# A fused sliding-window attention and gated feed-forward gradient kernel: score products two units ahead, transposed copies through DRAM, and other queues for the second half's loads

## The chip, the cores and the metric

The kernel runs on one core of a Trainium2 chip. The metric is the device time of one execution in microseconds (us). A core has TensorE (PE in the profile, with its weight loads apart as PEld), VectorE (DVE), ScalarE (ACT), GpSimd (POOL) and SyncE (SP). SP computes nothing here: it issues DMAs one after the other, and a DMA that has to wait for something holds back every DMA behind it on the same queue.

## The reference

The reference returns the output and all gradients of a gated sum of two branches, with 2048 positions, width 512 and bfloat16 data:

```python
g = sigmoid((x * gate_w).sum(-1, keepdims=True))
a = attention(x, wqkv, wo)       # 32 heads of 16, causal, window of 256 positions
b = (relu(x @ W_gate) * (x @ W_up)) @ W_down      # 1376 hidden columns
out = g * a + (1 - g) * b        # and the gradients to x, wqkv, wo, W_gate, W_up, W_down, gate_w
```

## The kernel before

The work has four parts in order of time.

**Prologue.** `x` and `grad_out` are loaded as rows and transposed on TensorE, the gate is computed, and `proj(0)` (L213) makes queries, keys, values and the projected output gradient of the first eight heads, which go through DRAM buffers `KV_d` and `QD_d`.

**Main loop** (L608 to L632). Eight groups of four heads times four blocks of 512 positions give 32 stages `n`. Each is visited twice: `A` with its queries against the keys in the window, and `N` with its keys against the queries. A visit has six units (L401): three packs of blocks, each for two heads of the four (`r` 0 or 1). This makes 384 units. A unit is: score matmuls into the PSUM tile `S` (L429), the exponential on ScalarE into `Pt` (L462), one or two mask instructions on GpSimd over `Pt` (L439), matmuls of the incoming gradient with the values into the PSUM tile `dP` (L429 too), and the product `Pd = Pt * dP` on VectorE (L467). `S` and `dP` have one buffer each. One step of the loop issues the `dP` matmuls of unit u woven with the `S` matmuls of unit u+1, then the exponential and masks of u+1, then the product of u. So the scores of a unit are one unit ahead of its product.

After the sixth unit of a visit the results are swept up on TensorE (L479) in small tasks (`tasks_A`, `tasks_N`), one per following step. `tasks_A` computes on VectorE `OB`, `Ar`, `V`, `tt`, on GpSimd `U`, `pr`, `dqO`, and turns `U` and `V` into rows with two transposing DMAs from SBUF to SBUF (L537, L538). `load_stage` (L377) loads the tiles of a later stage and transposes `kv` into `kvr` in the same way.

Each step also calls `fill` (L584). It takes one piece of a running `proj` (three of them are started, at `A` stages 0, 8 and 16) and as many pieces of the feed-forward part as keep that in step with the share of units done (`TOTAL` is its length in us as the code counts it). The feed-forward part works on 11 strips of 128 hidden columns (the last has 96). `ffn_front` (L243) makes, for each 512 positions, `rg` (ACT), `upm` (DVE), `hT` (POOL), `dhs` and `dgT` (DVE) and `duT` (POOL); it writes `hT`, `dgT`, `duT` to DRAM for the last part, and turns them into rows with 48 TensorE transposes per strip (L295) and six ScalarE copies `rw` (L296). `ffn_back` (L301) of the strip before reads those rows as matmul operands (L308, L318); the two generators alternate. The framework's scheduler then sets the order on each engine; it may move pieces past each other.

**Weight gradients of the attention** (L660 to L733, called part 5 below). Loads of `dqT`, `dkvT` and `OT` stand on SP's queue, and five weight loads on ScalarE's queue. 34 groups of TensorE transposes with a copy each (L685, L656, L658) turn the weights; then come four rounds of 16 tiles (L703).

**Output and input gradient** (L754 on, part 6): eight groups of two tiles, with `hT`, `dgT`, `duT` read back from DRAM.

## Time and profile before

| what | us |
|---|---|
| median of 4 runs (1236.8 to 1240.17) | 1238.53 |
| the profiled execution | 1245.8 |
| its span, first to last instruction | 1244.1 |
| before the first product | 50.6 |
| main loop, first to last product (50.6 to 891.6) | 841.0 |
| from there to the first matmul of the rounds (958.9) | 67.3 |
| the four rounds (to 1050.5) | 91.6 |
| part 6 (to the end) | 193.6 |

The profiled execution is 7.3 us above the median, and 1.7 us of its time lie outside its span. In a row of a group, `x` is the number of instructions, then busy time in us and the mean of one in ns, then the engine's idle time before them and what ended it. Rows of waits read "who <- for whom: us in total, times, longest". A chain of waits is followed back from the last instruction. `SPq` and `ACTq` are instructions that issue a DMA on SP's or ScalarE's queue: their time is that of the issue, not of the transfer.

### The profile page before, as it was taken

The numbers are of one execution on the slowest core, as the hardware profiler recorded it, in microseconds if no ns is written. First come the engines' busy times: TensorE is split into PE (matmuls) and PEld (weight loads), VectorE is DVE, ScalarE is ACT, GpSimd is POOL, SyncE is SP. The second block draws the span as 40 slices with busy tenths as digits, with TensorE's granted clock in tenths as the row PEclk, the third lists the DMA queues.
The fourth block names the chain that finished last, engine by engine and source line by source line (L and its number), as shares of the span: only waits on it lengthen the run. The fifth ranks groups of instructions, "written<-read, shape, count | busy, mean of one in ns | idle before, by whom it ended". The sixth has DMA issues, their size and how long they took to land.

```text
span 1244.1 us, 26168 instructions
## 1 busy us (share of the span) xinstructions
PE 1026.5 (83%) x10162; PEld 498.5 (40%) x10276; DVE 704.9 (57%) x876; ACT 619.7 (50%) x817; POOL 635.9 (51%) x1019
## 2 busy tenths in 40 slices
PE   5688888898788888888888888898706887899998
PEld 4234434444344343444434434344405443344443
DVE  2247777767677776678777776777402113223222
ACT  5256566675666666667676665666403222101110
POOL 2747766666676765667777665677401001122221
PEclk9889999899999999999999997999955999899999
DMA  7346232243232323323342332212395002834430
GB/s 194 90 121 148 76 87 65 58 125 87 68 88 65 89 71 98 103 60 87 76 90 63 72 83 65 65 36 53 100 233 207 17 18 77 243 102 151 126 102 22
DMA packets 191342, 117.57 MB, mean 95 GB/s; under 512 B 93489, under 2 KB 186066, under 8 KB 191218
## 3 DMA queue, kind: packets, MB, share of 16 engines
q1 hardware_dynamic: 160610, 89.78, 27.5%
q10 hardware_dynamic: 28224, 19.70, 5.6%
q0 software_dynamic: 2384, 6.43, 1.6%
q8 instruction: 80, 1.31, 0.4%
q14 instruction: 44, 0.36, 0.1%
HBM read 59.05 MB, written 44.21 MB: 83 GB/s over the span
## 4 chain that ended last, share of the span: by engine, by line
PE 34%; POOL 18%; DVE 15%; issue 10%; ACT 10%; DMA 9%; SPq 2%; ACTq 1%; DVEq 0%; POOLq 0%
DVE Pd L467 10%; POOL Pt L439 8%; PE dxps L804 7%; ACT Pt L462 4%; PE dP L429 4%; PE dw L719 4%; DMA dkvT<-DKV_d 3%; PE acc L479 3%; PE bps L771 2%; DMA duT_g<-duT_d 2%; PE mm L308 2%; POOL duT L287 2%; PE S L429 2%; POOL db_r L365 2%; POOL dqO L533 2%
## 5 line engine op out<-in xcount | busy, mean ns | idle before, releaser
L467 DVE TENSOR_TENSOR Pd<-Pt,dP 128x1024 bf16<-128x1024 bf16 (+2 forms) x384 | 442.6, 1153 | 199.7 <-POOL Pt L439 124.2
L462 ACT ACTIVATE Pt<-S 128x1024 bf16<-128x1024 f32 (+2 forms) x384 | 373.6, 973 | 228.8 <-PE S L429 201.0
L439 POOL TENSOR_SCALAR_AFFINE_SELECT Pt<-Pt 128x256 bf16<-128x256 bf16 (+1 forms) x736 | 347.4, 494 | 207.1 <-ACT Pt L462 203.9
L429 PE MATMUL dP<-dO,kv 32*128 32x128 bf16 (+2 forms) x704 | 77.0, 280 | 37.3 <-DVE Pd L467 33.2
L308 PE MATMUL mm<-rw,x_r 128*128 128x256 bf16 (+1 forms) x704 | 102.5, 277 | 0.8 <-ACT rw L296 0.8
L429 PE MATMUL dP<-kv,dO 32*128 32x384 bf16 (+2 forms) x704 | 73.5, 273 | 35.9 <-DVE Pd L467 33.6
L429 PEld LDWEIGHTS <-kv 32*128 32x128 bf16 x1408 | 47.0, 92 | 121.5 <-issue 112.5
L429 PE MATMUL S<-kv,Q 32*128 32x384 bf16 (+2 forms) x704 | 86.7, 275 | 6.8 <-ACT Pt L462 5.9
L778 ACT COPY a_sb<-aps 128x512 f32<-128x512 f32 x16 | 9.4, 586 | 161.3 <-issue 78.6
L429 PE MATMUL S<-Q,kv 32*128 32x128 bf16 (+2 forms) x704 | 84.1, 283 | 2.9 <-ACT Pt L462 1.6
L308 PEld LDWEIGHTS <-x_r 128*128 128x128 bf16 x704 | 61.5, 99 | 32.7 <-issue 21.0
L296 ACT COPY rw<-mmt 128x1024 bf16<-128x1024 bf16 (+1 forms) x66 | 65.1, 995 | 9.3 <-PE mmt L295 9.0
L804 PE MATMUL dxps<-WgT_sb,dgT_g 128*128 128x512 bf16 (+1 forms) x176 | 66.7, 379 | 0.8
L429 PEld LDWEIGHTS <-dO 32*128 32x128 bf16 x704 | 34.3, 91 | 79.3 <-issue 75.4
L711 POOL DMA_DIRECT2D go_t<-in_grad_out_dram x16 | 8.7, 544 | 112.1 <-DVE da_t L713 106.5
L287 POOL TENSOR_TENSOR duT<-dhs,rg 128x512 bf16<-128x512 bf16 (+1 forms) x44 | 54.3, 1235 | 17.4 <-DVE dhs L284 16.2
L804 PE MATMUL dxps<-WuT_sb,duT_g 128*128 128x512 bf16 (+1 forms) x161 | 61.0, 379 | 0.0
L277 POOL TENSOR_TENSOR hT<-rg,upm 128x512 bf16<-128x512 bf16 (+1 forms) x44 | 50.8, 1154 | 19.2 <-DVE upm L275 18.4
L227 PE MATMUL mm<-x_T,w 128*128 128x512 bf16 x180 | 51.0, 398 | 10.8 <-ACT cs L576 4.1
L719 PE MATMUL dw<-rt,x_r 128*128 128x512 bf16 x184 | 46.0, 387 | 12.3 <-ACT rt L656 11.8
L784 POOL DMA_DIRECT2D out_dram<-o_sb x16 | 8.7, 543 | 90.7 <-DVE o_sb L782 62.5
L782 DVE SCALAR_TENSOR_TENSOR o_sb<-bps,omg_all,ga 128x512 bf16<-128x512 f32 x16 | 12.0, 751 | 73.9 <-ACT ga L780 72.2
(155 smaller groups left out, 1686.3 us busy)
## 6 DMA issues: line engine op xcount, KB each, us to landing
hT_d<-hT SPq DMA_DIRECT2D x40, 128.0 KB
dgT_d<-dgT SPq DMA_DIRECT2D x40, 128.0 KB
duT_d<-duT SPq DMA_DIRECT2D x40, 128.0 KB
dgT_g<-dgT_d ACTq DMA_DIRECT2D x8, 640.0 KB
hT_g<-hT_d SPq DMA_DIRECT2D x8, 640.0 KB
duT_g<-duT_d ACTq DMA_DIRECT2D x8, 640.0 KB
KV_d<-cs SPq DMA_DIRECT2D x32, 128.0 KB
QD_d<-cs SPq DMA_DIRECT2D x32, 128.0 KB
```

What stands on the lines that cost most here:

```text
L227: nc.tensor.matmul(pp[:], lhsT=w3[:, cd, which, :], rhs=x_T[:, cd, sl], start=(cd == 0), stop=(cd == DC - 1))
L277: nc.gpsimd.tensor_tensor(out=hT[:fs, :], in0=rg[:fs, :], in1=upm[:fs, :], op=ALU.mult)
L287: nc.gpsimd.tensor_tensor(out=duT[:fs, :], in0=dhs[:fs, :], in1=rg[:fs, :], op=ALU.mult)
L296: nc.scalar.copy(rw[:, :, which, :fs], pt[:, :, :fs])
L308: nc.tensor.matmul(wps[:, 0:2 * fs], lhsT=x_r[:, t, c * P:(c + 1) * P], rhs=rows[t // 8][:, t % 8, 1:3, :fs], start=(t == 0), stop=(t == N ...
L429: lst.append(lambda lt=lt, ls=ls, rt=rt, rsl=rsl, i=i, rs=rs, col=col, cnt=cnt: nc.tensor.matmul(bank[:, i % 2, col * P:(col + cnt) * P], ...
L439: nc.gpsimd.affine_select(out=v.rearrange("p h (b k) -> p h b k", b=cnt), in_=v.rearrange("p h (b k) -> p h b k", b=cnt), compare_op=ALU.i ...
L462: nc.scalar.activation(u.Pt[:, :, :u.width], u.S[:, :, :u.width], ACT.Exp)
L467: nc.vector.tensor_tensor(out=u.Pd[:, :, :u.width], in0=u.Pt[:, :, :u.width], in1=u.dP[:, :, :u.width], op=ALU.mult)
L479: nc.tensor.matmul(acc[32 * i:32 * i + wt.shape[1], q0:q0 + cnt * P], lhsT=wt, rhs=m[:, i % 2, col * P:(col + cnt) * P], start=(fresh and ...
L719: nc.tensor.matmul(banks[c][:], lhsT=x_r[:, t, c * P:(c + 1) * P], rhs=rt[:].rearrange("p a b -> p (a b)"), start=(t == 0), stop=(t == NT ...
L804: nc.tensor.matmul(dxps[:], lhsT=l_, rhs=r_, start=(i == 0), stop=(i == len(pairs) - 1))
```

## The change

**Units.** The loop issues the scores two units ahead of the product: a step weaves `dP` of unit g-1 with `S` of unit g+1. The order of `r` in a visit becomes 0, 1, 1, 0, 0, 1 and is mirrored in every other visit; the two units of a step then use different rows of the TensorE array, as they did before. `Pt` has 10 buffers for 9; `U`, `V` and `OB` one for two. `S` and `dP` keep one buffer each.

**Feed-forward rows.** The TensorE transposes and their ScalarE copies are gone. `hT`, `dgT`, `duT` are written to one DRAM tensor `ffn_d`, and right behind the three writes one transposing DMA reads a 384 x 512 block of it back as rows (three of 96 x 512 each in the last strip). It has to wait until the three writes have landed. `TOTAL` goes from 262 to 229.

**Attention rows.** `U` and `V` are written to DRAM (`UV_d`), and one transposing DMA reads both back; `kvr` is made from `KV_d` in DRAM and not from `kv` in SBUF.

**Pacing.** A running `proj` gives a piece at every second step, not at every one, and its `cs` has four buffers for two. `load_stage(n + 2)` comes one step later, behind the product.

**Part 5.** The five weight loads move from ScalarE's queue to SP's; three stand ahead of `dqT`, and `Wd` and `wo` behind `OT`.

```diff
-            for hf in range(NSB // 2):
...
-                rw = fp.tile([P, 8, 3, P], BF, tag="rows", bufs=3)
-                for which in range(3):
-                    pt = tr_bank(8)
-                    for k in range(8):
-                        nc.tensor.transpose(pt[:, k, :fs], parts[k // 4][which][:fs, (k % 4) * P:(k % 4 + 1) * P], ident[:fs, :fs])
-                    nc.scalar.copy(rw[:, :, which, :fs], pt[:, :, :fs])
+            for tg in range(NSB):
...
+                for w, src_t in enumerate((hT, dgT, duT)):
+                    nc.sync.dma_start(ffn_d[fc, w, :fs, sl], src_t[:fs, :])
+                rw = fp.tile([P, 4, 3, P], BF, tag="rows", bufs=6)
+                if fs == P:
+                    nc.sync.dma_start_transpose(out=rw[:].rearrange("p k w f -> p k (w f)"),
+                                                in_=ffn_d[fc, :, :, sl].rearrange("w p s -> (w p) s"))
+                else:
+                    for w in range(3):
+                        nc.sync.dma_start_transpose(out=rw[:, :, w, :fs], in_=ffn_d[fc, w, :fs, sl])
...
-            transpose_rows(kvr, kv)
+            nc.sync.dma_start_transpose(out=kvr[:], in_=KV_d[c][sb][half * P:(half + 1) * P, :])
...
-                transpose_rows(RU, v.U)
-                transpose_rows(RV, v.V)
+                nc.sync.dma_start(UV_d[n][0], v.U[:])
+                nc.sync.dma_start(UV_d[n][1], v.V[:])
+                R = ap_.tile([P, 4, 2, P], BF, tag="R", bufs=3, name="R")
+                nc.sync.dma_start_transpose(out=R[:].rearrange("p k w f -> p k (w f)"),
+                                            in_=UV_d[n].rearrange("w p s -> (w p) s"))
...
         def fill(frac):
-            if projs:
+            turn[0] += 1
+            if projs and turn[0] % 2:
...
-            lists = second(u)
-            if nxt is not None:
-                lists = lists + first(nxt)
+            lists = (second(cur[4]) if cur else []) + (first(nxt[4]) if nxt else [])
             weave(lists)
             if nxt is not None:
-                after_scores(nxt)
-            product(u)
+                after_scores(nxt[4])
+            if cur is not None:
+                kind, n, us, j, u = cur
+                product(u)
...
-            nc.scalar.dma_start(Wg_sb6[:], B_W_gate.rearrange("(c p) f -> p c f", p=P))
-            nc.scalar.dma_start(Wu_sb6[:], B_W_up.rearrange("(c p) f -> p c f", p=P))
-            nc.scalar.dma_start(wqkv_sb6[:], A_wqkv.rearrange("(c p) n -> p c n", p=P))
+            nc.sync.dma_start(Wg_sb6[:], B_W_gate.rearrange("(c p) f -> p c f", p=P))
+            nc.sync.dma_start(Wu_sb6[:], B_W_up.rearrange("(c p) f -> p c f", p=P))
+            nc.sync.dma_start(wqkv_sb6[:], A_wqkv.rearrange("(c p) n -> p c n", p=P))
```

What this does to the order on the engines shows at three places. The first is VectorE in the middle of the main loop. Numbers are given to tiles in the order in which the code makes them. Before, `Pt_7022` is made just before the product `Pd_7026` and read by the very next product:

```order
L467 TENSOR_TENSOR Pd_7026<-Pt_6994,dP_7012 128x1024
L275 SCALAR_TENSOR_TENSOR upm_7071<-rg_7010,mm_7066 128x512
L467 TENSOR_TENSOR Pd_7057<-Pt_7022,dP_7043 128x1024
L467 TENSOR_TENSOR Pd_7102<-Pt_7053,dP_7088 128x1024
L467 TENSOR_TENSOR Pd_7152<-Pt_7098,dP_7138 128x1024
```

In the change `Pt_8057` is made just before `Pd_8060`, and another product stands between that and the one that reads it:

```order
L462 TENSOR_TENSOR Pd_8060<-Pt_7949,dP_8049 128x1024
L504 SCALAR_TENSOR_TENSOR OB_8099<-acc_8062,vec_154,ri_8003 128x512
L462 TENSOR_TENSOR Pd_8097<-Pt_7973,dP_8087 128x2x256
L462 TENSOR_TENSOR Pd_8132<-Pt_8057,dP_8122 128x2x256
L270 SCALAR_TENSOR_TENSOR upm_8141<-rg_8047,mm_8136 128x512
```

`Pt` moved one product further ahead; `dP` is still made for the next product alone.

The second place is SP's queue in the main loop. Before, writes, loads and single-block transposes alternate, and none of them reads what another of them has just written to DRAM:

```order
L534 DMA DQO_d<-dqO 128x512
L385 DMA Q_4_597<-QD_d_2_82 16x512 x2
L381 DMA kv<-KV_d_2_66 128x512
L386 DMA dO_4_602<-QD_d_2_82 16x512 x2
L289 DMA hT_d<-hT 128x512
```

In the change the transposing read `rw<-ffn_d` follows the last write of its block, `dgT`, with four small loads between:

```order
L284 DMA ffn_d<-duT 128x512
L284 DMA ffn_d<-dgT 128x512
L380 DMA Q_0_623<-QD_d_2_112 16x512 x4
L287 DMA_TRANSPOSE rw<-ffn_d 128x4x384
L532 DMA UV_d_65<-V 128x512
L172 DMA wg<-in_B_W_gate_dram 128x4x128
```

Whatever stands behind that read on the queue now waits until the write has landed.

The third place is ScalarE's queue where part 5 begins. Before, its first copy of transposed weights stands behind the issue of all five loads (`Wd` in two pieces):

```order
L674 DMA Wg_sb_15073<-in_B_W_gate_dram 128x4x1376
L323 CAST dst<-mm 96x512
L675 DMA Wu_sb_15074<-in_B_W_up_dram 128x4x1376
L676 DMA wqkv_sb_15075<-in_A_wqkv_dram 128x4x1536
L677 DMA Wd_sb_15047<-in_B_W_down_dram 128x10x512
L679 DMA Wd_sb_15047<-in_B_W_down_dram 96x512
L680 DMA wo_sb_15050<-in_A_wo_dram 128x4x512
L656 COPY WgT_sb<-pt 128x512 x5
```

In the change no load stands ahead of that copy on ScalarE, and SP's queue reads:

```order
L668 DMA dqT<-DQO_d 128x1x2048
L663 DMA Wg_sb_14501<-in_B_W_gate_dram 128x4x1376
L664 DMA Wu_sb_14502<-in_B_W_up_dram 128x4x1376
L665 DMA wqkv_sb_14503<-in_A_wqkv_dram 128x4x1536
L668 DMA dqT<-DQO_d 128x1x2048 x2
L670 DMA dkvT<-DKV_d 128x2048 x8
```

The loads of part 5 moved from two queues to one, with two of the four pieces of `dqT` ahead of the weights.

More of the change, by code (lines that the diff above doesn't have):

```diff
@@ L317, in ffn_back @@
             for t in range(NT):
-                nc.tensor.matmul(dps[:fs, :D], lhsT=rows[t // 8][:, t % 8, 0, :fs], rhs=db_r[:, t, :],
+                nc.tensor.matmul(dps[:fs, :D], lhsT=rows[t // 4][:, t % 4, 0, :fs], rhs=db_r[:, t, :],
                                  start=(t == 0), stop=(t == NT - 1))
@@ L549, in f @@
                     d, k = divmod(a - 4 * sb, 4)
[L550 removed]
+                    return st["rn", n + d][:, k, which, 32 * i:32 * i + width]
                 return f
@@ L576, in act_copy @@
             nc.scalar.copy(out, in_)
-        slots = sum(len(units(k, n)) for k, n in order)
         dense = {"done": 0.0, "t": 0.0}
         ffn = ffn_all()
-        TOTAL = 262.0
+        TOTAL = 229.0
         projs = []
+        turn = [0]
         def fill(frac):
-            if projs:
+            turn[0] += 1
+            if projs and turn[0] % 2:
                 try:
@@ L597 @@
             load_stage(n)
[L598 to L601 removed]
         seq = []
[L603 removed]
+        for kind, n in order:
+            us = units(kind, n)
             for j, u in enumerate(us):
                 seq.append((kind, n, us, j, u))
[L606 to L611 removed]
+        pending = []
+        for g in range(-1, len(seq) + 1):
+            nxt = seq[g + 1] if g + 1 < len(seq) else None
+            cur = seq[g - 1] if g >= 1 else None
+            if nxt is not None and nxt[0] == "A" and nxt[3] == 0:
+                n = nxt[1]
+                if n % 8 == 0 and n // 8 + 1 < DC:
                     projs.append(proj(n // 8 + 1, act_copy))
@@ L658, in evac @@
                 nc.vector.tensor_copy(out, in_)
-        dqo_v = DQO_d.rearrange("(c g w d) s -> w c g d s", c=DC, g=8, w=2)
-        for c in range(DC):
-            nc.sync.dma_start(dqT[:, c, :], dqo_v[0, c])
-        for hg in range(NHG):
-            nc.sync.dma_start(dkvT[:, hg, :], DKV_d[hg * P:(hg + 1) * P, :])
-        for c in range(DC):
-            nc.sync.dma_start(OT[:, c, :], dqo_v[1, c])
         with ExitStack() as p5:
```

165 lines of the change are left out of this document (75 added, 90 removed).

## The prediction

> **What bounds the kernel now.** I read the stretches first, cut at the first product, the last product and the first and last matmul of the rounds. Columns are start:end, length, then busy time of PE, PEld, DVE, ACT and POOL, then the granted TensorE clock, the DMA share and GB/s.
>
> ```profile
> 50.60:891.60 841.00, 720.70 (x8453) 344.99 (x8538) 609.78 (x660) 545.51 (x693) 558.03 (x918) 0.98 0.31 80
> 891.60:958.90 67.30, 23.42 (x176) 18.37 (x176) 8.44 (x21) 12.12 (x22) 7.81 (x11) 0.57 0.85 234
> 958.90:1050.50 91.60, 75.16 (x493) 40.31 (x503) 22.32 (x51) 21.26 (x38) 4.86 (x9) 0.98 0.11 35
> 1050.50:1244.10 193.60, 177.04 (x787) 76.80 (x800) 52.15 (x115) 19.61 (x34) 36.70 (x48) 0.98 0.40 123
> ```
>
> Part 6 keeps PE busy 91% of its time, and the change gives it the same matmuls and the same row lengths: I leave its 193.6 us and the rounds' 91.6 as they are. What is left is the main loop, where no engine is full, and the 67.3 us behind it, where PE works a third of the time.
>
> In the loop I asked who waits for whom.
>
> ```profile
> POOL Pt L439 <- ACT Pt L462: 203.9, 203, 4.5
> ACT Pt L462 <- PE S L429: 201.0, 229, 3.9
> DVE Pd L467 <- POOL Pt L439: 124.2, 151, 5.4
> PE dP L429 <- DVE Pd L467: 66.8, 155, 1.7
> ```
>
> That is a ring: the product waits for the masks, these for the exponential, this for the scores; and the scores are woven with `dP` matmuls that wait for the product before. Since the scores are one unit ahead, the ring closes over two products. If I remove it, the next ring is the short one of `dP` alone, and VectorE's timeline shows its length.
>
> ```profile
> 833.37 1.22 DVE L467 TENSOR_TENSOR Pd<-Pt,dP 128x1024 bf16<-128x1024 bf16 x1 [0.58 <-PE dP L429]
> 834.51 0.74 DVE L517 SCALAR_TENSOR_TENSOR Ar<-acc,vec,ri 128x512 f32<-128x512 f32 x1
> 835.17 0.68 DVE L275 SCALAR_TENSOR_TENSOR upm<-rg,mm 96x512 bf16<-96x512 bf16 x1
> 835.76 1.21 DVE L467 TENSOR_TENSOR Pd<-Pt,dP 128x1024 bf16<-128x1024 bf16 x1
> ...
> 841.12 1.21 DVE L467 TENSOR_TENSOR Pd<-Pt,dP 128x1024 bf16<-128x1024 bf16 x1
> 842.25 0.74 DVE L528 SCALAR_TENSOR_TENSOR tt<-acc,vec,OB 128x512 f32<-128x512 f32 x1
> 842.91 1.22 DVE L467 TENSOR_TENSOR Pd<-Pt,dP 128x1024 bf16<-128x1024 bf16 x1
> ```
>
> A product cannot follow the one before by less than 0.58 us, while `dP` is refilled. One other operation fits into that gap (841.12 to 842.91 is 1.79, less 1.21 is 0.58); two make it 1.18 (833.37 to 835.76, less 1.22), and I take 2.0 for three or more by the same spacing. `dP` keeps its one buffer, so this floor stays.
>
> **The floor and the room above it.** The products themselves:
>
> ```profile
> L467 DVE TENSOR_TENSOR Pd<-Pt,dP 128x1024 bf16<-128x1024 bf16 (+2 forms) x384 | 442.6, 1153 | 199.7 <-POOL Pt L439 124.2 <-PE dP L429 40.2 <-PE S L429 24.0
> ```
>
> In the change's order on VectorE, of the 383 gaps between products 185 are empty, 134 hold one operation, 55 two and 9 more. The floor is 442.6 + 319 x 0.58 + 55 x 1.18 + 9 x 2.0 = 711 us, or 1.85 per product. The loop takes 841, so its whole room is 130 us. Where that lies shows when the same stretches are asked for the products alone (length, then DVE busy and count of products, clock, DMA share, GB/s; a product across a border counts twice):
>
> ```profile
> 50.60:128.00 77.40, 27.78 (x25) 0.93 0.49 123
> 128.00:226.00 98.00, 55.20 (x48) 1.00 0.29 75
> 226.00:282.50 56.50, 27.72 (x25) 0.94 0.37 96
> 282.50:436.30 153.80, 82.99 (x73) 0.99 0.31 80
> 436.30:547.60 111.30, 55.30 (x49) 1.00 0.32 85
> 547.60:741.80 194.20, 110.61 (x96) 1.00 0.33 77
> 741.80:798.30 56.50, 27.67 (x24) 0.82 0.23 60
> 798.30:891.60 93.30, 55.29 (x48) 1.00 0.18 48
> ```
>
> With 24, 48, 24, 72, 48, 96, 24 and 48 products at 1.85, the excess is 33, 9, 12, 21, 22, 17, 12 and 4 us. The start has 33. The stretches with a running `proj` (the third, the head of the fourth, the fifth) have about 45. The seventh has 12 at a granted clock of 0.82. Plain stretches have about 40.
>
> **The change part by part.**
>
> *Scores two units ahead.* The exponential:
>
> ```profile
> L462 ACT ACTIVATE Pt<-S 128x1024 bf16<-128x1024 f32 (+2 forms) x384 | 373.6, 973 | 228.8 <-PE S L429 201.0
> ```
>
> The long ring then closes over three products. Its own length, from the end of a product: 0.97 for the exponential and 1.22 for the product by their rows, and as my estimates 0.5 for the scores, 1.0 for two masks and 0.3 of handing over, about 4.0: 2.0 per product over two, 1.33 over three, below the 1.8 of the short ring. So the mask waits go, and the `dP` wait is late next. POOL is the releaser of 124.2 of the 199.7 us for which VectorE idles, but of each such wait 0.58 would be there anyway. In the plain stretches I take half of the 40 back (bounds 0 and 35): -22. At the start the loads of the first stages bind as well: -15 of 33 (0 to 25).
>
> *Pacing of `proj`, four `cs` buffers.* A ScalarE copy into `cs` waits for the write two copies before, on the engine that makes the exponentials. In the chain two such writes stand whole:
>
> ```profile
> 72.63 3.12 DMA KV_d<-cs
> 498.06 2.63 DMA QD_d<-cs
> ```
>
> They run from issue to landing. With four buffers and half the pace a write has four times as long, and the wait goes: -27 of the 45 (10 to 35). The clock dip I leave in, since nothing in the change speaks to it.
>
> *TensorE transposes and their copies gone.* Rows of the loop stretch for L295 (PE, PEld) and the group of L296:
>
> ```profile
> 50.60:891.60 841.00, 46.49 (x528) 33.27 (x528) 0.98 0.31 80
> L296 ACT COPY rw<-mmt 128x1024 bf16<-128x1024 bf16 (+1 forms) x66 | 65.1, 995 | 9.3 <-PE mmt L295 9.0
> ```
>
> PE loses 46.5 us and ACT 65.1, but both are idle for over 100 us of the loop now, and neither is the floor: 0 by itself, and part of what makes the terms above possible.
>
> *Rows through DRAM.* Two costs, both on SP. First its time. Median issues now (min/median/max in ns):
>
> ```profile
> L396 SPq DMA_TRANSPOSE RU<-U x32: 1189/1192/1945, 84.3 to 859.3; - x32
> L289 SPq DMA_DIRECT2D hT_d<-hT x44: 304/358/956, 75.0 to 875.7; - x44
> L388 SPq DMA_DIRECT2D qd<-QD_d x32: 327/571/1436, 46.4 to 787.5; - x32
> ```
>
> Up to part 5 the change's order has 732 plain DMAs and 116 transposes of 225 blocks of 128 x 512 (before: 669 and 96). Some 690 plain ones fall into the loop, at 0.45 (between the rows) 310 us. No row shows a transpose out of DRAM: from below it is a plain issue, 116 x 0.36 = 42; from above it is 1.19 for every block, 268. Then 84 groups of transposes wait for their own writes, 2.6 to landing less the issues between, at most 1.8 each: 150. The sum is 450 to 728 of a loop of 785. I take the upper end, since the only transposes in the trace cost 1.19: SP stays hidden, without reserve. The Trainium skill (Advanced Engine Details and Errata, X-Bar Transpose) says that transposing DMAs are as fast as regular ones on this chip. For the issue the row speaks against it, 1.19 to 0.36; by the rule SP's sum would be the lower end and the time the same.
>
> Second, latency. By the change's order five other units' `dP` stand on PE between the last gradient matmul of a strip (it feeds `dhs`) and the first matmul that reads the rows of that last block: 5 x 2.0 = 10 us.
>
> ```profile
> L287 POOL TENSOR_TENSOR duT<-dhs,rg x44: 1148/1156/1414, 75.4 to 876.4; 128x512 bf16<-128x512 bf16 x40, 96x512 bf16<-96x512 bf16 x4
> ```
>
> In that time must pass `dhs` (0.68), a wait for a product (0.6), `duT` (1.16), SP's queue (0.5), the write (2.6 to 3.1) and the transposing read (2.6 as a plain one, 5.8 with two more block issues): 8.1 to 11.8 us. What is missing stalls PE and all that stands behind it there, `dP` first: 0 to 2 us on each of 10 strips. I take 8 of 0 to 20.
>
> *Attention rows, `load_stage` one step later, fewer `U`, `V`, `OB` buffers.* 0: the rows of `U` and `V` are read some 12 units after the transpose is issued, over 20 us, and the loads serve a stage two ahead. If SP fell behind, this cover would go too; that is a rival below.
>
> Loop: 841 - 22 - 15 - 27 + 8 = 785.
>
> *Part 5.* TensorE's timeline behind the loop:
>
> ```profile
> 894.68 1.89 PE L318 MATMUL mm<-db_r,rw 128*96 128x512 bf16 x8
> ...
> 902.68 1.01 PE L685 MATMUL pt<-ident,Wg_sb 128*128 128x128 bf16 x8 [6.11 <-DMA Wg_sb<-in_B_W_gate_dram]
> ```
>
> and that of all engines and queues:
>
> ```profile
> 899.72 40.77 SPq L664 DMA_DIRECT2D dkvT<-DKV_d  x8
> ...
> 919.97 0.37 ACTq L677 DMA_DIRECT2D Wd_sb<-in_B_W_down_dram  x1
> ...
> 937.20 0.44 ACTq L680 DMA_DIRECT2D wo_sb<-in_A_wo_dram  x1
> 937.68 1.07 ACT L656 COPY WgT_sb<-pt 128x512 bf16<-128x512 bf16 x2 [40.50 <-DMA dkvT<-DKV_d]
> ...
> 957.68 1.01 PE L685 MATMUL pt<-ident,dqT 128*128 128x128 bf16 x8 [0.25 <-ACT wkvT L656]
> ```
>
> ScalarE's first copy comes at 937.68 behind the issue of `wo`, 40.5 us late; the 34 groups then take 20 us (937.7 to 957.7). In the change ScalarE issues nothing here. Counted from 896.6, where PE ends the loop's leftovers: ahead of `Wg` stands half of `dqT` (1.0 MB), then `Wg` 1.4, `Wu` 1.4, `wqkv` 1.6 MB. At 234 GB/s they are there after 11, 17 and 24 us. GpSimd's reordering of `wqkv` takes 4 us, the last eight groups 5: rounds from 33, now 62 (958.9). The half of `dqT` left needs 4 us more of transfer, by 28: in time. Bounds 10 (a copy still waits for a late transfer) to 32; I take 26.
>
> Sum: 1245.8 - 56 - 26 = 1163.8; less 7.3, by which the profiled execution lies above the median, 1157.
>
> **The rivals.** (a) *The rows come late.* Stalls of 5 us and more per strip take back the loop's whole gain; part 5 alone stays: 1238.5 - 26 = 1212. For it: the path needs up to 11.8 of 10 us. Against it: only the last block of a strip is tight, the third has 13 units. (b) *Part 5 is bound by transfers.* 67.3 us at 234 GB/s are 15.7 MB, the same bytes after. If the first copies still wait for late pieces, only the loop gains: 1157 + 26 = 1183. The Trainium skill (DMA: Bandwidth & Descriptors, Issuing engines are not separate DMA queues) has it that the DMAs of all queues share the same engines, and that another queue saves issue time alone. Against it: what ScalarE waited for at 937.68 was not the weights, and PE had `Wg` at 902.7. (c) *SP becomes the bound, slower.* If a block out of DRAM costs 2.0 us of SP's time and not 1.19, the queue needs 310 + 450 + 150 = 910 us, the loads come late and the loop follows: +69 - 26, 1281. It decides from 1.8 a block (310 + 150 + 225 x 1.8 = 865, 24 above the loop of now). For it: the upper sum has no reserve, and a transposing issue took up to 1.9 us now and then (`RU`, above). Against it: DRAM reads as such issue in 0.36 to 0.57. (d) *Nothing comes of it:* the new waits eat all, 1238.
>
> **How the numbers follow.** Forecast 0.60, (a) 0.14, (b) 0.10, (c) 0.13, (d) 0.03. The range goes from 1110, where the loop comes within 25 us of its floor, to 1225, beyond (a): outside lie (c), (d) and a little below, under 2 in 10. About 0.2% is what a measurement can tell from no change. Faster 0.84, same 0.03, slower 0.13.
>
> **What would show it.** Right: VectorE's waits for POOL's masks nearly gone, `dP` in their place, products 1.80 apart in plain stretches; 384 products in some 785 us; the first `WgT` copy about 12 us and the rounds about 33 us after PE's last loop matmul. Wrong: transposing issues on SP well over 1.2 us a block, or waits of L303 for `rw` in the tens of us, or `S` and the exponential still releasing the product.

## The result and the profile after

| | us |
|---|---|
| before, median of 15 runs | 1242.38 |
| changed, median of 11 runs (1142.7 to 1155.08) | 1153.06 |
| ratio, 95% interval | 0.9266 (0.9235 to 0.9296) |
| changed, profiled execution (span 1141.0) | 1142.7 |

The forecast was 1157 in a range of 1110 to 1225. The profiled execution lies 10 us below the median; how executions of one kernel differ is taken up at the last experiment. First the stretches of the changed kernel, cut at the same events as before: first product, last product, first and last matmul of the rounds.

```profile
49.80:817.90 768.10, 679.32 (x7892) 312.63 (x8002) 611.87 (x656) 486.73 (x624) 554.86 (x918) 0.99 0.48 120
817.90:856.70 38.80, 18.86 (x151) 15.50 (x150) 8.52 (x22) 11.61 (x20) 7.84 (x11) 0.56 0.89 281
856.70:948.70 92.00, 75.18 (x494) 39.98 (x503) 22.64 (x52) 21.76 (x39) 4.86 (x9) 0.98 0.27 85
948.70:1141.00 192.30, 177.77 (x784) 76.93 (x800) 51.67 (x115) 19.11 (x33) 36.70 (x48) 0.97 0.40 124
```

The loop went from 841.0 to 768.1 (785 forecast), the stretch behind it from 67.3 to 38.8 (41.3 forecast); the other two stayed within 1.3 us. VectorE is busy in the loop as long as before, 612 us beside 610; the time came out of its gaps. Who waits for whom in the changed kernel:

```profile
ACT Pt L457 <- PE S L424: 178.7, 243, 3.5
POOL Pt L434 <- ACT Pt L457: 140.6, 167, 4.3
DVE Pd L462 <- PE dP L424: 70.3, 110, 3.5
DVE Pd L462 <- PE S L424: 37.6, 47, 8.7
DVE Pd L462 <- POOL Pt L434: 10.1, 12, 1.7
```

The product's wait for the masks fell from 124.2 to 10.1. ScalarE and GpSimd still wait long, 178.7 and 140.6, but now a unit ahead, where the product seldom stands right behind them. What is late next is `dP`, as forecast. The waits put down to `S` grew from 24.0 to 37.6; 38 of the 47 are no longer than 0.65 us, which is the gap of the short ring (the scores are woven with `dP` in one step), and one, of 8.7, belongs to late rows and comes up again at `hybrid_last`. VectorE's timeline in the middle of the loop shows the short ring at its length:

```profile
565.17 1.22 DVE L462 TENSOR_TENSOR Pd<-Pt,dP 128x1024 bf16<-128x1024 bf16 x1 [0.60 <-PE dP L424]
566.97 1.22 DVE L462 TENSOR_TENSOR Pd<-Pt,dP 128x1024 bf16<-128x1024 bf16 x1 [0.58 <-PE dP L424]
568.11 0.68 DVE L270 SCALAR_TENSOR_TENSOR upm<-rg,mm 128x512 bf16<-128x512 bf16 x1
568.74 1.22 DVE L462 TENSOR_TENSOR Pd<-Pt,dP 128x1024 bf16<-128x1024 bf16 x1
```

Starts are 1.80 and 1.77 apart, with and without another operation in the gap. Now the products alone, in stretches that hold the same products as the eight of before (columns as there):

```profile
49.80:113.30 63.50, 27.61 (x24) 0.92 0.63 156
113.30:207.60 94.30, 55.27 (x48) 1.00 0.52 127
207.60:255.70 48.10, 27.64 (x24) 1.00 0.52 134
255.70:397.00 141.30, 82.95 (x73) 1.00 0.50 122
397.00:497.30 100.30, 55.23 (x49) 1.00 0.49 126
497.30:678.10 180.80, 110.51 (x96) 1.00 0.48 119
678.10:723.50 45.40, 27.61 (x24) 1.00 0.48 117
723.50:817.90 94.40, 55.24 (x48) 0.98 0.29 71
```

| stretch | before | after | |
|---|---|---|---|
| start | 77.4 | 63.5 | -13.9 |
| second | 98.0 | 94.3 | -3.7 |
| third, `proj` | 56.5 | 48.1 | -8.4 |
| fourth, `proj` at its head | 153.8 | 141.3 | -12.5 |
| fifth, `proj` | 111.3 | 100.3 | -11.0 |
| sixth | 194.2 | 180.8 | -13.4 |
| seventh, clock 0.82 before | 56.5 | 45.4 | -11.1 |
| eighth | 93.3 | 94.4 | +1.1 |

SP's transposing issues, whose price the prediction could only bound (min/median/max in ns), for three blocks, two and one of 128 x 512:

```profile
L287 SPq DMA_TRANSPOSE rw<-ffn_d x40: 1293/1414/2322, 69.4 to 730.8; - x40
L534 SPq DMA_TRANSPOSE R<-UV_d x32: 1232/1251/2863, 83.9 to 789.0; - x32
L385 SPq DMA_TRANSPOSE kvr<-KV_d x32: 1194/1208/2032, 49.5 to 691.3; - x32
```

At the median one such issue costs 1.21 us for one block, 0.04 more for two and 0.20 more for three. With the last strip's 12 (median 1.19) all 116 come to 40 x 1.41 + 32 x 1.25 + 32 x 1.21 + 12 x 1.19 = 149 us, where the prediction had 42 to 268 and took 268.

Part 5, all engines and queues behind the loop:

```profile
825.10 0.40 SPq L663 DMA_DIRECT2D Wg_sb<-in_B_W_gate_dram  x1
...
833.96 1.01 PE L681 MATMUL pt<-ident,Wg_sb 128*128 128x128 bf16 x8 [15.46 <-DMA Wg_sb<-in_B_W_gate_dram]
834.63 0.59 ACT L653 COPY WgT_sb<-pt 128x512 bf16<-128x512 bf16 x1 [15.24 <-PE pt L681]
```

ScalarE's first copy now comes 0.7 us behind the first transpose, and not behind the issue of five loads; the transposes wait 15.5 us for `Wg`.

### The profile page after: what moved, and what is told of

Its sections match the earlier page's. It is cut to its first block, busy times and chain, and to the rows that moved or that the text cites. A ratio compares the mean times of both kernels' runs of the same rounds, so it can differ in the third digit from the quotient of the medians.

```text
span 1141.0 us, 25063 instructions
## 1 busy us (share of the span) xinstructions
PE 984.7 (86%) x9607; PEld 465.1 (41%) x9748; DVE 709.7 (62%) x876; ACT 562.7 (49%) x751; POOL 632.7 (55%) x1019
## 3 DMA queue, kind: packets, MB, share of 16 engines
q8 instruction: 76, 1.25, 0.5%
## 5 line engine op out<-in xcount | busy, mean ns | idle before, releaser
L457 ACT ACTIVATE Pt<-S 128x1024 bf16<-128x1024 f32 (+2 forms) x384 | 372.6, 970 | 197.2 <-PE S L424 178.7
L434 POOL TENSOR_SCALAR_AFFINE_SELECT Pt<-Pt 128x256 bf16<-128x256 bf16 (+1 forms) x736 | 348.0, 496 | 146.5 <-ACT Pt L457 140.6
L303 PE MATMUL mm<-rw,x_r 128*128 128x256 bf16 (+1 forms) x704 | 102.2, 274 | 10.3 <-DMA rw<-ffn_d 10.0
L424 PEld LDWEIGHTS <-kv 32*128 32x128 bf16 x1408 | 55.7, 92 | 114.6 <-issue 104.9
L424 PE MATMUL dP<-dO,kv 32*128 32x128 bf16 (+2 forms) x704 | 74.3, 273 | 27.4 <-DVE Pd L462 24.5
L424 PE MATMUL S<-kv,Q 32*128 32x384 bf16 (+2 forms) x704 | 78.5, 276 | 2.6 <-ACT Pt L457 1.4
L424 PE MATMUL S<-Q,kv 32*128 32x128 bf16 (+2 forms) x704 | 78.1, 275 | 2.8 <-ACT Pt L457 1.9
L303 PEld LDWEIGHTS <-x_r 128*128 128x128 bf16 x704 | 60.6, 98 | 44.8 <-issue 31.5
L424 PEld LDWEIGHTS <-dO 32*128 32x128 bf16 x704 | 30.1, 92 | 72.3 <-issue 69.2
L779 POOL DMA_DIRECT2D out_dram<-o_sb x16 | 8.7, 542 | 90.1 <-DVE o_sb L777 62.4
L715 PE MATMUL dw<-rt,x_r 128*128 128x512 bf16 x184 | 45.9, 387 | 12.7 <-ACT rt L653 12.2
L282 POOL TENSOR_TENSOR duT<-dhs,rg 128x512 bf16<-128x512 bf16 (+1 forms) x44 | 51.4, 1168 | 6.9 <-DVE dhs L279 6.4
L225 PE MATMUL mm<-x_T,w 128*128 128x512 bf16 x175 | 48.6, 386 | 3.9 <-issue 1.9
L653 ACT COPY rt<-pt 128x512 bf16<-128x512 bf16 x32 | 18.8, 588 | 65.7 <-PE pt L681 65.7
```

The lines of the kernel that those rows point to most:

```text
L225: nc.tensor.matmul(pp[:], lhsT=w3[:, cd, which, :], rhs=x_T[:, cd, sl], start=(cd == 0), stop=(cd == DC - 1))
L282: nc.gpsimd.tensor_tensor(out=duT[:fs, :], in0=dhs[:fs, :], in1=rg[:fs, :], op=ALU.mult)
L303: nc.tensor.matmul(wps[:, 0:2 * fs], lhsT=x_r[:, t, c * P:(c + 1) * P], rhs=rows[t // 4][:, t % 4, 1:3, :fs], start=(t == 0), stop=(t == N ...
L424: lst.append(lambda lt=lt, ls=ls, rt=rt, rsl=rsl, i=i, rs=rs, col=col, cnt=cnt: nc.tensor.matmul(bank[:, i % 2, col * P:(col + cnt) * P], ...
L434: nc.gpsimd.affine_select(out=v.rearrange("p h (b k) -> p h b k", b=cnt), in_=v.rearrange("p h (b k) -> p h b k", b=cnt), compare_op=ALU.i ...
L457: nc.scalar.activation(u.Pt[:, :, :u.width], u.S[:, :, :u.width], ACT.Exp)
```

## The experiments

The theory is the prediction's: a ring of masks, exponential and scores over two products bound the loop, writes of `cs` held `proj`, and ScalarE's issues held part 5; transposes on TensorE and their replacement are off the path. The rivals: the transposes made the gain; part 5 is bound by transfers; SP or the rows come close to binding. Ratios are to the kernel before, on the same chip in the same rounds. The changed kernel itself was timed in a second set as well, `same_again`:

> The changed kernel as it is, for a second profile on the chip of the two below: 1148 to 1157. Its first profiled execution took 1142.7, 10 under the median of 1153. If that was the clock, this one shows more stretches of granted clock 0.5 in the loop, and as much more time there; if it was something else, the loop is longer at the same clock.

It gave a median of 1146.51, ratio 0.9234 (0.9202 to 0.9266), and a profile of 1145.0 with a loop of 770.0: as fast as the first profile, so that it left the question open which it was meant for. Where a run is set against the changed kernel below, that counts as the mean of the two ratios, 0.925, and a difference of ratios is turned into us by 1240.

| run | median | ratio, 95% interval | against changed |
|---|---|---|---|
| `one_ahead` | 1192.38 | 0.9635 (0.9594 to 0.9675) | +48 |
| `pe_rows` | 1151.14 | 0.9321 (0.9280 to 0.9362) | +9 |
| `proj_old` | 1169.40 | 0.9446 (0.9416 to 0.9477) | +24 |
| `cs_two` | 1159.72 | 0.9334 (0.9301 to 0.9367) | +10 |
| `act_loads` | 1178.14 | 0.9499 (0.9466 to 0.9532) | +31 |
| `act_three` | 1166.22 | 0.9403 (0.9373 to 0.9433) | +19 |
| `split_three` | 1182.06 | 0.9523 (0.9489 to 0.9558) | +34 |
| `hybrid_last` | 1153.92 | 0.9298 (0.9254 to 0.9341) | +6 |
| `part5_chain` | 1137.20 | 0.9185 (0.9151 to 0.9220) | -8 |
| `b_two_ahead` (from before) | 1202.05 | 0.9703 (0.9677 to 0.9730) | |
| `b_part5` (from before) | 1215.31 | 0.9778 (0.9743 to 0.9813) | |

**`one_ahead`**: the distance of the scores undone.

```diff
-            for k, r in enumerate((0, 1, 1, 0, 0, 1)):
+            for k, r in enumerate((0, 1, 0, 1, 0, 1)):
...
-                u.kind, u.n, u.p, u.r, u.width, u.base = kind, n, k // 2, r ^ (stage_no["n"] % 2), width * P, base
+                u.kind, u.n, u.p, u.r, u.width, u.base = kind, n, k // 2, r, width * P, base
...
-        for g in range(-1, len(seq) + 1):
+        for g in range(-1, len(seq)):
...
-            cur = seq[g - 1] if g >= 1 else None
+            cur = seq[g] if g >= 0 else None
```

> The changed kernel with its scores one unit ahead again (a step weaves dP of unit u with S of unit u+1, and r runs 0, 1, 0, 1, 0, 1); all else as changed. The changed kernel takes 1153. Theory (the ring of masks, exponential and scores bound the loop, and the second unit of distance opens it): VectorE's waits for POOL's masks come back from 10 us to 100 or more, the dP waits shrink, and the two terms of the prediction, 22 in the plain stretches and up to 15 at the start, are lost: 1175 to 1190. Rival (the transposes taken from PE and ACT made the gain, and the distance is worth nothing): 1150 to 1158, the masks' waits staying below 40 us.

48 us are lost, more than the 37 expected. The waits of the product in it, by releaser:

```profile
DVE Pd L462 <- PE dP L424: 82.0, 111, 2.1
DVE Pd L462 <- POOL Pt L434: 60.6, 60, 6.0
```

The masks' waits are back, to 60.6 and not to the 100 and more expected, with PE and ACT free of the transposes. The theory holds; that the transposes made the gain does not. Its loop takes 812.5 us at a mean granted clock of 0.97; by the working shown at `split_three` some 25 of the 44 us more are waits, and the rest came with the lower clock.

**`b_two_ahead`**: the same distance put alone into the kernel before, with the changed kernel's loop, `units` and `sweep`.

```diff
-            u.Pt = ap_.tile([P, 2, W], BF, tag="Pt", bufs=9, name="Pt")
+            u.Pt = ap_.tile([P, 2, W], BF, tag="Pt", bufs=10, name="Pt")
...
-                v.OB = ap_.tile([P, W], BF, tag="OB", bufs=2, name="OB")
+                v.OB = ap_.tile([P, W], BF, tag="OB", bufs=1, name="OB")
...
-            lists = second(u)
-            if nxt is not None:
-                lists = lists + first(nxt)
+            lists = (second(cur[4]) if cur else []) + (first(nxt[4]) if nxt else [])
```

> The kernel before with one part of the change alone: scores two units ahead, the order of r that goes with it, ten Pt buffers, load_stage behind the product (OB has one buffer for two, so that it fits into SBUF); transposes, proj, rows and part 5 as before. The kernel before takes 1240. Theory (the ring alone): 22 to 37 us less, 1203 to 1218, the masks' waits of the product down from 124 us to under 40. Rival (the distance pays only where PE and ACT were first freed of the transposes): 1228 to 1242, the mask waits replaced by waits for S, the exponential or dP of the same size.

The gain is 0.0297 x 1240 = 37 us, with all 528 transposes in place. Its waits, and the products of the start, the third and the seventh stretch:

```profile
DVE Pd L470 <- PE dP L432: 61.2, 90, 2.8
DVE Pd L470 <- PE S L432: 55.5, 74, 4.5
DVE Pd L470 <- POOL Pt L442: 13.7, 14, 5.3
```

```profile
50.70:130.90 80.20, 27.65 (x25) 0.91 0.46 120
221.30:275.90 54.60, 27.66 (x25) 1.00 0.38 99
708.90:754.70 45.80, 27.64 (x25) 1.00 0.31 80
```

The mask waits are gone here too. But the start took 80.2 (77.4 before), so alone the distance does nothing there; and the seventh stretch lost its dip in the clock with this part alone.

**`pe_rows`**: the rows by TensorE and ScalarE again.

```diff
-                    nc.sync.dma_start_transpose(out=rw[:].rearrange("p k w f -> p k (w f)"),
-                                                in_=ffn_d[fc, :, :, sl].rearrange("w p s -> (w p) s"))
...
+                for which in range(3):
+                    pt = tr_bank(8)
+                    for k in range(8):
+                        nc.tensor.transpose(pt[:, k, :fs], parts[k // 4][which][:fs, (k % 4) * P:(k % 4 + 1) * P], ident[:fs, :fs])
+                    nc.scalar.copy(rw[:, :, which, :fs], pt[:, :, :fs])
+                    yield 0.5
...
-        TOTAL = 229.0
+        TOTAL = 262.0
```

> The changed kernel with the feed-forward rows made by 528 TensorE transposes and 66 ScalarE copies again (TOTAL 262, three row tiles of twice the size); the three writes go to ffn_d, but nothing is read back from there in the loop. Theory of the prediction (the transposes are off the critical path, and the way through DRAM costs some 8 us of late rows): 1145 to 1155. Rival (with the ring opened PE is the next to bind: it is busy 679 of the 768 us of the loop, and has no room for 46 more, nor ACT for 65 ahead of the exponentials): 1175 to 1200, with S and the exponential releasing the product more often.

It is 9 us slower, by intervals that overlap with those of the changed kernel's first set and not of its second: at the edge of what can be told. The loop:

```profile
51.30:817.80 766.50, 690.44 (x8432) 333.86 (x8521) 609.92 (x656) 541.39 (x690) 554.52 (x918) 0.99 0.38 98
```

766.5 beside 768.1: the loop is as long whether TensorE and ScalarE or DMAs do this work. The rival that PE would bind fell.

**`hybrid_last`**: only the last block of a strip by TensorE, the three before it through DRAM.

```diff
+                if tg == NSB - 1:
+                    for w, src_t in enumerate((hT, dgT, duT)):
+                        pt = tr_bank(4)
+                        for k in range(4):
+                            nc.tensor.transpose(pt[:, k, :fs], src_t[:fs, k * P:(k + 1) * P], ident[:fs, :fs])
+                        nc.scalar.copy(rw[:, :, w, :fs], pt[:, :, :fs])
+                        yield 0.25
-                if fs == P:
+                elif fs == P:
...
-        TOTAL = 229.0
+        TOTAL = 237.0
```

> The changed kernel with the rows of the last block of each strip, the fourth, made by 12 TensorE transposes and three ScalarE copies from SBUF, and those of the first three through DRAM as changed (TOTAL 237). Theory (only the last block of a strip comes late through DRAM; its 12.5 us of waits for rw are what the transposes' 46.5 us of PE were traded for, so that the two ways come out even): the waits for rw go to under 2 us, and the time is 5 to 12 under the changed kernel's, 1141 to 1148. Rival (a wait of PE for rw is covered, since the product's short ring binds): 1150 to 1156, the waits gone and the loop as long.

My expectation fell. The matmuls that read the rows no longer wait, in the changed kernel (L303) 10.3 us, here (L310) 0.8:

```profile
L303 PE MATMUL mm<-rw,x_r 128*128 128x256 bf16 (+1 forms) x704 | 102.2, 274 | 10.3 <-DMA rw<-ffn_d 10.0
```

```profile
L310 PE MATMUL mm<-rw,x_r 128*128 128x256 bf16 (+1 forms) x704 | 101.9, 275 | 0.8 <-DVE cs L236 0.6
51.00:820.20 769.20, 677.64 (x8016) 317.49 (x8119) 608.69 (x656) 503.30 (x656) 554.65 (x918) 0.98 0.45 114
820.20:863.80 43.60, 22.52 (x165) 17.13 (x164) 8.53 (x22) 12.03 (x21) 7.80 (x11) 0.57 0.90 231
```

The loop stays at 769.2. That does not show that the ten us were covered: 6.5 of them are a single wait in the start of the changed kernel, and the product stands behind it:

```profile
104.41 1.01 PE L303 MATMUL mm<-rw,x_r 128*128 128x256 bf16 x4 [6.48 <-DMA rw<-ffn_d]
106.10 1.22 DVE L462 TENSOR_TENSOR Pd<-Pt,dP 128x1024 bf16<-128x1024 bf16 x1 [8.71 <-PE S L424]
```

Without it the start took 59.7 us in `hybrid_last` and 57.5 in `pe_rows`, where the changed kernel took 63.5. In `hybrid_last` the second stretch lost as much again: 98.2 at a granted clock of 0.97, for 94.3 at 1.00. By its interval the run can't be told from the changed kernel. Behind the loop it took 43.6 for 38.8; 3.2 of this are loop matmuls that PE still works off after the last product (3.8 us, in the changed kernel 0.6).

**`split_three`**: the same reads, each issued as three.

```diff
-                if fs == P:
-                    nc.sync.dma_start_transpose(out=rw[:].rearrange("p k w f -> p k (w f)"),
-                                                in_=ffn_d[fc, :, :, sl].rearrange("w p s -> (w p) s"))
-                else:
-                    for w in range(3):
-                        nc.sync.dma_start_transpose(out=rw[:, :, w, :fs], in_=ffn_d[fc, w, :fs, sl])
+                for w in range(3):
+                    nc.sync.dma_start_transpose(out=rw[:, :, w, :fs], in_=ffn_d[fc, w, :fs, sl])
```

> The changed kernel with each transposing read of feed-forward rows issued as three of one 128 x 512 block instead of one of three: the same bytes, 80 more transposing issues. In the changed kernel's profile a transposing issue takes SP 1.21 us for one block, 1.25 for two and 1.41 for three: so this adds 40 x (3 x 1.2 - 1.41) = 88 us to SP, and some 2.2 us to the way of each block. Theory (SP has over 200 us of waits in the loop left, and the rows come in time): 1150 to 1160. Rival (SP or the way of the rows is close to binding, as the prediction's upper sum had it): 1165 to 1200, with waits of L303 for rw well over the 12.5 us of now.

The rival is right: 34 us slower.

```profile
L299 PE MATMUL mm<-rw,x_r 128*128 128x256 bf16 (+1 forms) x704 | 107.9, 282 | 30.4 <-DMA rw<-ffn_d 30.2
51.20:859.90 808.70, 698.62 (x7894) 315.11 (x8004) 612.97 (x656) 487.17 (x624) 555.18 (x918) 0.96 0.45 114
```

The waits for rows went from 10.0 to 30.2, and the loop grew by 40.6. The rest goes with the clock: length times mean granted clock, with the clock as the traces record it (0.958 and 0.991), is 774 here and 761 in the changed kernel, 13 more; the other 27 came with the lower clock. (That this product is the length at full clock is an estimate; `part5_chain` below shows what speaks for it.) So the rows' way through DRAM has no room for three issues in place of one, some 88 us more by the medians above. SP is not full for that: it waits for other engines and DMAs 263 us in this loop, and 327 in the changed kernel's. Each block's way got longer.

**`proj_old`** and **`cs_two`**: both edits to `proj` undone, and the buffers alone.

```diff
-                    cs = wp.tile([P, W], BF, tag="cs", bufs=4)
+                    cs = wp.tile([P, W], BF, tag="cs", bufs=2)
...
-            if projs and turn[0] % 2:
+            if projs:
```

> The changed kernel with a proj piece at every step and two cs buffers, as before the change. Theory of the prediction (the ScalarE copy into cs waits for the write two copies before and holds the exponentials; 27 us, bounds 10 to 35): 1163 to 1188, the loss in the stretches with a running proj. Rival (with scores two ahead such a wait is covered by the unit in hand): 1150 to 1160.

> The changed kernel with two cs buffers for four; the half pace of proj stays. With both undone the loss was 2% (22 us). Theory (at half the pace the write two copies before has landed, so the pacing is what pays): 1153 to 1158. Rival (the buffers are what pays; the write waits in SP's queue behind the transposing reads): 1165 to 1175.

24 and 10 us are lost (13, if `cs_two` is set against the 1146.51 of its own set): the term of 27 is there, about half of it in the buffers. But not where the prediction had it. The start in `proj_old`, then its third stretch:

```profile
51.60:134.00 82.40, 27.62 (x25) 0.92 0.57 145
...
224.30:276.80 52.50, 27.65 (x25) 1.00 0.52 133
```

and the start in `cs_two`:

```profile
50.90:125.10 74.20, 27.59 (x25) 0.89 0.60 145
```

Against 63.5 that is 19 and 11 us in the first 24 products, where the first of the three `proj` runs beside the first loads; the third stretch (48.1 changed) loses 4 in `proj_old`. In the start of `proj_old` the copies into `cs` on ScalarE and VectorE wait 17 us for the writes to `KV_d` and `QD_d`, in the changed kernel's not at all, so the mechanism is the prediction's. In `cs_two` it is 3 us only, and what the other 8 are is open.

**`act_loads`** and **`act_three`**: all part 5 weight loads on ScalarE's queue again, and only the first three. The edit of `act_three` is shown; `act_loads` moves `Wd` and `wo` in the same way.

```diff
-            nc.sync.dma_start(Wg_sb6[:], B_W_gate.rearrange("(c p) f -> p c f", p=P))
-            nc.sync.dma_start(Wu_sb6[:], B_W_up.rearrange("(c p) f -> p c f", p=P))
-            nc.sync.dma_start(wqkv_sb6[:], A_wqkv.rearrange("(c p) n -> p c n", p=P))
+            nc.scalar.dma_start(Wg_sb6[:], B_W_gate.rearrange("(c p) f -> p c f", p=P))
+            nc.scalar.dma_start(Wu_sb6[:], B_W_up.rearrange("(c p) f -> p c f", p=P))
+            nc.scalar.dma_start(wqkv_sb6[:], A_wqkv.rearrange("(c p) n -> p c n", p=P))
```

> The changed kernel with all part 5 weight loads on ScalarE's queue again; all else as changed (1153). Theory (ScalarE's first copy stands behind the issue of Wd and wo, which waits for earlier transfers): the first WgT copy comes some 25 us later than the changed kernel's 834.6, with the clock at half speed for some 60 us as before the change, and the time is 1153 + 26 = 1179, bounds 1165 to 1185. Rival (part 5 is bound by its transfers, whose bytes are the same on either queue): 1150 to 1160.

> The changed kernel with Wg, Wu and wqkv alone on ScalarE's queue; Wd and wo stay on SP's behind OT. Theory (only Wd and wo, at the end of ScalarE's queue, hold its copies; the first three don't): the first copy follows Wg within 1 us, and the time is that of the changed kernel or up to 8 us less, since Wg need not stand behind SP's dqT pieces: 1145 to 1155. Rival (any of these issues on ScalarE's queue delays the copies; the issue of wqkv waits as well): 1160 to 1180, the first copy over 10 us behind Wg.

`act_loads` gives all of the term back, 31 us; counted from the last product its first copy comes 33 us later than the changed kernel's, and not 25. `act_three` gives 19 of it back, against the theory, though its first copy follows `Wg` at once, as the theory said. All engines in `act_three`:

```profile
829.19 0.46 ACTq L663 DMA_DIRECT2D Wg_sb<-in_B_W_gate_dram  x1
...
851.92 1.01 PE L681 MATMUL pt<-ident,Wg_sb 128*128 128x128 bf16 x8 [29.58 <-DMA Wg_sb<-in_B_W_gate_dram]
852.54 0.59 ACT L653 COPY WgT_sb<-pt 128x512 bf16<-128x512 bf16 x1 [29.33 <-PE pt L681]
```

and in `act_loads`:

```profile
833.55 0.45 ACTq L663 DMA_DIRECT2D Wg_sb<-in_B_W_gate_dram  x1
857.91 1.01 PE L681 MATMUL pt<-ident,Wg_sb 128*128 128x128 bf16 x8 [31.44 <-DMA Wg_sb<-in_B_W_gate_dram]
874.37 0.83 ACTq L676 DMA_DIRECT2D wo_sb<-in_A_wo_dram  x1
875.24 1.07 ACT L653 COPY WgT_sb<-pt 128x512 bf16<-128x512 bf16 x2 [47.90 <-DMA wqkv_sb<-in_A_wqkv_dram]
```

Two things differ. From the issue of `Wg` to its first use pass 22.7 us and 24.4 us when SP issues `dqT` and `dkvT` beside it, and 8.9 when `Wg` stands ahead of most of these on one queue. And in `act_loads` alone ScalarE's copies stand another 17.3 us behind the issue of `wo`. The Trainium skill (DMA: Bandwidth & Descriptors, Issuing engines are not separate DMA queues) says that the DMAs of all engines run on the same 16 DMA engines and interleave; the 22.7 against 8.9 agree.

**`b_part5`**: the part 5 edit alone in the kernel before (as in the diff of the change).

> The kernel before with one part of the change alone: the part 5 loads on SP's queue in the change's order (1240 before). Theory: 26 us less, 1214 (bounds 1208 to 1230), all of it between the last product and the first matmul of the rounds, 67.3 us there down to about 40. Rival (transfers bind): 1233 to 1243.

0.0222 x 1240 = 28 us: as forecast. In its profile the stretch behind the loop went from 67.3 to 42.7.

**`part5_chain`**: an attempt at a better version, read from the chain of part 5.

```diff
-            nc.sync.dma_start(Wg_sb6[:], B_W_gate.rearrange("(c p) f -> p c f", p=P))
+            for f0, f1 in ((0, 4 * P), (4 * P, F)):
+                nc.sync.dma_start(Wg_sb6[:, :, f0:f1], B_W_gate[:, f0:f1].rearrange("(c p) f -> p c f", p=P))
...
-                pt = ps5.tile([P, 8, P], BF, tag="tr", bufs=2)
+                pt = ps5.tile([P, 8, P], BF, tag="tr", bufs=3)
...
-                banks = [ps5.tile([P, D], F32, tag="dw", bufs=6, name="dw") for _ in range(DC)]
+                banks = [ps5.tile([P, D], F32, tag="dw", bufs=5, name="dw") for _ in range(DC)]
```

> The changed kernel with the load of Wg in two halves by columns and three transpose buffers for two in PSUM (five banks for the rounds' results, not six). In the changed kernel's chain stand one after the other the write of the last dkv (5.6 us to landing), Wg (8.6), and 34 groups in pairs of 1.26 us, TensorE and the copies in turn. Theory: the first copy comes about 4 us after less (the first half lands 4 us sooner), the pairs go to 1.0 to 1.1, and wqkv with its reordering, which ends at 847, holds the last eight groups: 4 to 8 us from the stretch between the last product and the rounds, now 38 to 39. In all 1145 to 1149 where the changed kernel takes 1153, or 0.3 to 0.7% less than its ratio. Rival (transfers: what is gained at the first copy is waited for again at wqkv and dqT; five banks cost waits between rounds): 1151 to 1157.

It is faster than the kernel before, and by 8 us than the changed one, at the edge of what can be told: the interval of 0.9185 ends below the changed kernel's first and overlaps with that of the second. Its stretches:

```profile
50.90:835.50 784.60, 693.13 (x7894) 317.13 (x8006) 612.23 (x656) 487.25 (x625) 554.05 (x920) 0.97 0.47 117
835.50:870.70 35.20, 15.78 (x154) 13.03 (x153) 8.33 (x21) 11.36 (x20) 7.88 (x11) 0.67 0.90 285
870.70:950.50 79.80, 74.16 (x492) 39.67 (x500) 22.15 (x52) 20.98 (x39) 5.09 (x9) 0.97 0.35 109
```

3.6 us came from the stretch I aimed at, where the three edits are not told apart; the rival was right in part, as PE waits 3.2 us for `dqT` there. 12.2 came from the rounds (92.0 to 79.8), which I had not expected: they use the same transpose buffers, and PE's waits for ScalarE's copies in them fell from 16.3 to 2.3 us. The loop, whose code is untouched, took 784.6 here and 768.1 in the changed kernel's profile. Length times granted clock is 760 and 761. `same_again`, `act_three` and `act_loads` have the same loop too: 770, 771 and 775 us, 761 to 763 by the clock. So these executions of one loop differ by the clock that was granted, by up to 16 us, and that is more than several edits here are worth; what lowers the clock is not shown. Nor does every difference go with the clock: the run at the changed kernel's median, 1153.06, has the same mean clock as the profiled one, 0.973. This is why kernels were set against each other by rounds, and profiles only by stretch.

## Why the prediction was right

The sign was right, and the time within 4 us: 89 us by the medians, where 82 were forecast. In the profiled executions it is 103, with 73 from the loop and 28.5 from part 5 (56 and 26 forecast). That the medians agree so closely is in part luck, as errors of single steps cancel. By its steps:

*Scores two ahead* (22, and 15 at the start). Right in kind: the mask waits went and `dP` came next. The sum of 37 is what `b_two_ahead` gained (48 when undone), but by luck in part: there the start gave nothing of its 15, the fourth stretch gave 14 (153.8 to 139.9) and the seventh 11, by its clock. Wrong in place: the 15 at the start are for the most part not its own. With this part alone the start took 80.2, and with the two `proj` edits undone 82.4; `proj` runs there as well, which the step had overlooked. With `proj` paced the distance does bring something there (70.0 in `one_ahead`, below, for 63.5).

*Pacing and `cs`* (27). 24 measured, 19 of them at the start. The stretches that the step named gained 8 to 13 each, but not from the pacing alone. In the third, before took 56.5, the scores alone 54.6, the pacing without them 55.0 (`one_ahead`), both 48.1: it takes both. In the fourth it is the scores: 153.8 before, 139.9 with them alone, 149.4 without them. In the fifth `one_ahead` took 104.6 and `proj_old` 105.6, where before took 111.3 and the changed kernel 100.3.

*The clock dip left in* (0). Failed: 11 us came from the seventh stretch. If each stretch's length is taken times what its clock lacks to 1, some 20 us of the loop were lost to the clock before and 7 after: 13 of the loop's 73 us are a term that the prediction put at nothing, and the other 60 stand against its 56. The stretch takes 45.4 in the changed kernel, 45.8 with the scores alone, and 45.4 without them in `one_ahead`, of which these are the start, the third and the seventh:

```profile
50.60:120.60 70.00, 27.63 (x24) 0.90 0.58 148
222.00:277.00 55.00, 27.66 (x24) 0.88 0.42 108
725.60:771.00 45.40, 27.65 (x24) 1.00 0.45 112
```

So it isn't the distance alone that removes the dip; what in the old order made the clock fall there stays open. "Nothing in the change speaks to it" was no argument: the change altered the work of PE in every stretch.

*Transposes gone* (0). Right as far as is seen: the loop is 766.5 with them and 768.1 with the way through DRAM in their place.

*Rows through DRAM* (+8, 0 to 20). The size of the waits was right (10.0) by luck: the step had up to 2 us on each of ten strips, the trace has 6.5 in one wait in the start and 3.6 in the rest of the loop. (For the transposing read the step had 2.6 to 5.8 us; ahead of that wait it took 3.7 from issue to use.) In `hybrid_last`, without them, the start was 4 us shorter and the loop as long. Over all the way through DRAM is worth 0 to 9 us, not a loss. SP's sum was taken at its upper end and was wrong there: a transposing issue has a price each and not by block, and SP waits for other engines and DMAs in 327 of the loop's 768 us. (The lower end of 450 does not follow from its terms: 310 + 42 is 352 without waits for the writes, and 502 with the 150.) What had little reserve was not SP but the way of the rows: issued block by block, at 1.2 us each, the same reads cost 34 us. That is short of rival (c), which needed 1.8 us a block and a full queue. The Trainium skill (Advanced Engine Details and Errata, X-Bar Transpose) has transposing DMAs as fast as regular ones; for the issue the runs say otherwise, 1.2 us to 0.36.

*Part 5* (26). 28 alone, 31 undone. For the kernel before, the mechanism was right: `Wg` was used on PE 6.1 us behind its last loop matmul, and ScalarE's first copy came 35 us behind that. Put back into the changed kernel, the loads cost in two ways: 12 of the 31 are the queue that ScalarE's copies stood in, 19 (`act_three`) the order in which bytes arrive, which the step had not priced. Two of its signs came late: the first copy 16.1 us behind PE's last loop matmul and the rounds 38.2, where it had 12 and 33. From there the gain is 24 (62.4 to 38.2); the rest of the 28.5 is that PE had 5.0 us of loop matmuls left after the last product before and 0.6 after. Rival (b) held that the same bytes take the same time; but those needed first came first. It has a point for what is left: in `pe_rows` the first copy comes 7.7 us behind PE's last loop matmul, and the rounds still 37.6, as PE then waits 10.1 us for `dqT`.

*Attention rows, later `load_stage`, fewer buffers* (0). No run undid these by themselves, so this stays open. In the changed kernel GpSimd waits 10.1 us until the write of `U` has left its one buffer.

Undone singly, the four parts cost 48, 24, 9 and 31, in sum 112; the change brought 93. So some us come only with two parts together: in the start 6.5 are lost without the distance and 18.9 without the pacing, where both and all else brought 13.9.

## What to carry to other kernels

Work taken from engines that were not on the path brought nothing here, though it was a large part of the diff: find the ring that closes last, and lengthen its distance before anything else. A trace tells which wait is there, not what it costs, so check a wait by taking it away: without ten us of waits for rows the loop was as long, with thirty it was 41 us longer. Which queue a load stands in also decided when its bytes arrived: `Wg` took 22.7 us from issue to use or 8.9.

## What was not expected of the hardware

A transposing DMA costs its queue 1.21 us for one block of 128 x 512, 1.25 for two and 1.41 for three, so further blocks in one issue cost little. The same loop took 768.1 us at a granted clock of 0.99 and 784.6 at 0.97. In `part5_chain` a third transpose buffer in PSUM at the price of a result bank shortened the rounds from 92.0 to 79.8 us, and TensorE's idle time in them from 17 to 6 us.
